# x^T k of the first attention layer by seven block products instead of eight full ones, its key sums on TensorE, and weight scans as flat rows

## The chip, the cores and the metric

The kernel runs on one core of one Trainium2 chip. The metric is the device time of one execution in microseconds; the time before is the median of three runs.

The core has five engines with a queue each: TensorE (PE; PEld is its weight load), VectorE (DVE), ScalarE (ACT), GpSimd (POOL) and SyncE (SP). DMA transfers are issued from the queues of SP, ACT and POOL. Each queue is worked off in program order.

## The reference

Four layers on one sequence of 2048 rows of 1024 features: linear attention (A), gated block (B), and the same two once more with the same weights.

```python
phi = lambda t: jnp.where(t > 0, t + 1, jnp.exp(t)) + 1e-6
# A, on layernorm(x):
q, k, v = x @ wqkv                       # 32 heads of 32
kv  = einsum("bhsd,bhse->bhde", phi(k), v)
z   = einsum("bhsd->bhd", phi(k))
num = einsum("bhqd,bhde->bhqe", phi(q), kv)
den = einsum("bhqd,bhd->bhq", phi(q), z) + 1e-6
x   = x + (num / den) @ wo
# B, on layernorm(x):
x   = x + ((x @ w_gate) * (x @ w_up)) @ w_down
```

## The kernel before

**Tiles.** The 2048 rows are 16 tiles of 128 (t). A product is a group of matmuls of 128 x 128 by 128 x 512 into PSUM. PSUM is eight banks, used as four pairs, QP[0] to QP[3]. The instructions of all engines are written out by hand in one program order, and the framework adds the waits for data and buffers. A step stands in the queue of each of its engines at the place where its call is made.

**kv without v.** k^T v is computed as (x^T k)^T wv: first x^T k, summed over all rows (1024 x 1024, held in XK), then its product with wv by blocks (kv_unit), masked to the heads. So v is never made.

**Layer A, first time (layer_A(0)).** The key stage makes phi(k) for the 16 tiles. For each tile: statistics on VectorE (ln_stats: bn_stats, bn_aggr, then two small POOL operations), the normed tile (ln_apply on VectorE, or ln_apply_act: a POOL operation for the offset, then ACT), its transposition by a DMA on SP (tx), 16 matmuls (k_tile), and phi: exp on ACT, min and max on VectorE, the last one from PSUM. `units` lists these steps, two half tiles (index i) per tile; the lines under `for i, (t, n)` place everything else by i.

Next, xk_pair(c) makes 128-row blocks of x^T k two at a time: 2 x 16 matmuls over all tiles, and one copy on ACT. There are eight. Meanwhile sum_unit adds up the 16 key tiles in float32 on VectorE (sk), and z_parts and z_unit turn that into the sum over all 2048 rows, repeated in every partition (zb), by a matmul with ones.

Then come the query tiles (q_tile). The first eleven are woven with the remaining xk_pairs. A query tile issues 16 matmuls into a pair of banks, phi, and some steps of `later`: den_sums (phi(q) times zb, summed per head) and den_divide, whose result is transposed by DMA for the output product. With split set, ACT also reads PSUM for the x + 1 side of phi, and VectorE reads SBUF alone. Then kv_unit, the last five query tiles with kvo_unit (kv times wo), and 16 output tiles (out_tile: 16 matmuls, one add to X on VectorE). `jobs` places the norms and other preparations for layer B between the output tiles.

**Layer A, second time (layer_A(2)).** It uses block products: a 2 x 2 block scheme with seven products instead of eight. x_product(p, jp, pair) issues half of product p (16 matmuls), xsums and tsums make the sums of blocks of x and of keys on VectorE in 16-bit, x_add adds a saved product to the one in PSUM, and ACT saves products 1, 6 and 7. Layer B works by the same scheme.

**Scales.** The 16-bit float format of the block sums needs scales for the weights. They are powers of two from the weights' sums of squares. scan_fetch loads 512 KB of w_gate, w_up or w_down, and scan_step squares it on ACT with a sum (42 of them); scale_sum, scale_pow (a matmul with ones for the sum over partitions), scale_root (POOL pow) and scale_bits make the factors fac, key_scale what phi of scaled keys needs. scan_key squares the key weights for the fourth factor. scan_buf gives each scan its buffer; a fetch waits until the square of the buffer's earlier scan is done.

**Down weights.** down_prep(u) loads a piece of w_down, scales it, makes its block sums and stores them (WD). Pieces 0 and 1 are made between output tiles, the rest in the first pass of layer B, one for each of its units.

Of the kernel before, what the change touches and what calls it, by code (L numbers as in the profile page):

```python
# [38 lines left out]
def kernel(  # L39
# [45 lines left out]
    QP = [QQ[:, 2 * i:2 * i + 2, :] for i in range(4)]  # L85
    WZ = [dram.tile([P, D + 64], F32, name=f"WZ{i}")[:, 0:D] for i in range(4)]
# [7 lines left out]
    def tail(i, j):  # L94
# [12 lines left out]
    sk = K[0][:, HEAD:HEAD + 2 * D].bitcast(F32)  # L107
# [6 lines left out]
    scan_b = [W[:, 6 * D:8 * D], K[0][:, HEAD:HEAD + 2 * D]]  # L114
    scan_c = [K[i][:, HEAD:HEAD + 2 * D] for i in (4, 0, 1, 2, 3)]
# [11 lines left out]
          for b in (K[3][:, 0:2 * D], K[3][:, 2 * D:4 * D], K[6][:, 0:2 * D], K[6][:, 2 * D:4 * D], W[:, 6 * D:8 * D])]  # L127
# [6 lines left out]
           for b in (K[0][:, HEAD:HEAD + 2 * D], MX[:, 2 * D:4 * D], W[:, 0:2 * D], W[:, 2 * D:4 * D], K[4][:, 0:2 * D])]  # L134
    sk2, zhi, zlo = MX[:, 2 * D:4 * D].bitcast(F32), W[:, 5 * D:6 * D], MX[:, D:2 * D]
# [66 lines left out]
    kq = const.tile([P, 4], F32, tag="kq", name="kq")  # L202
    kap = const.tile([P, 1], F32, tag="kap", name="kap")
    part = const.tile([P, 4], F32, tag="part", name="part")
    partb = const.tile([P, 4], BF16, tag="partb", name="partb")

    def scan_src(i):
        m, c = divmod(i, NU)
        if m < 2:
            f, kh = divmod(c, 2)  # L210
            return wgu_v[m][:, kh * KH:(kh + 1) * KH, f * NB:(f + 1) * NB], KH
        return wd_v[:, 2 * c:2 * c + 2, :], 2
# [3 lines left out]
    EARLY, MID = 26, 33  # L216
    scan_buf = [scan_a[i % 4] for i in range(18)] + [(scan_a + scan_b[:1])[i % 5] for i in range(18, EARLY)]
    scan_buf += [scan_b[(i + 1) % 2] for i in range(MID - EARLY)] + [scan_c[i % 5] for i in range(NSCAN - MID)]
    scanned = [0, 0, 0]

    def scan_fetch():

        while scanned[1] < scanned[2]:
            i = scanned[1]
            if any(scan_buf[j] is scan_buf[i] for j in range(scanned[0], i)):
                return
            src, k = scan_src(i)
            (nc.sync if i < 14 else nc.gpsimd).dma_start(out=scan_buf[i].rearrange("p (k n) -> p k n", k=k), in_=src)
            scanned[1] += 1

    def scan_step(n=1):

        for _ in range(n):
            i = scanned[0]
            m, c = divmod(i, NU)
            nc.scalar.activation(out=scan_buf[i], in_=scan_buf[i], func=ACT.Square, accum_out=acc[:, m, c:c + 1])  # L236
            scanned[0] += 1
            if i == EARLY - 1:
                load_qkv(wv, 2)
            elif i == EARLY - 2:  # L240
                scanned[2] = MID
            scan_fetch()

# [4 lines left out]
    def scale_pow(lo, hi):  # L248

        ps = mm_tile()  # L250
        nc.tensor.matmul(out=ps[:, lo:hi], lhsT=ones[:], rhs=partb[:, lo:hi], start=True, stop=True)
        nc.vector.tensor_scalar(out=part[:, lo:hi], in0=ps[:, lo:hi], scalar1=1e-30, scalar2=None, op0=ALU.max)
        if hi == 4:
            nc.vector.tensor_scalar(out=part[:, 3:4], in0=part[:, 3:4], scalar1=2.0 ** -10, scalar2=None, op0=ALU.max)
# [4 lines left out]
    def scale_bits(lo, hi):  # L259
# [6 lines left out]
        if hi == 4:  # L266
# [4 lines left out]
    def key_scale():  # L271
# [9 lines left out]
                                op0=ALU.mult, op1=ALU.add)  # L281

# [119 lines left out]

    def proj_mm(t, w, ps, mid=None, at=KD // 4):
# [21 lines left out]
    def xk_pair(c):  # L425

        n, j = divmod(2 * c, KD)
        bank = []

        def part(ts):  # L430
            if not bank:
                bank.append(mm_pair())
            for i in range(2):
                for t in ts:
                    nc.tensor.matmul(out=bank[0][:, i, :], lhsT=xn_a[t][:, (j + i) * P:(j + i + 1) * P],
                                     rhs=pk[t][:, n * NB:(n + 1) * NB], start=(t == 0), stop=(t == NT - 1))

        def end():
            part(range(NT - 2, NT))
            nc.scalar.copy(out=XK[n][:, j:j + 2, :], in_=bank[0])  # L440
        return [lambda: part(range(NT - 2)), end]

    def sum_unit(t):

        def run():
            nc.vector.tensor_tensor(out=sk, in0=pk[0] if t == 1 else sk, in1=pk[t], op=ALU.add)
        return run

    zparts = []

    def z_parts():

        hi = turn("pq", pqb)
        lo = turn("pq", pqb)
        nc.scalar.copy(out=hi, in_=sk)
        nc.vector.tensor_tensor(out=lo, in0=sk, in1=hi, op=ALU.subtract)
        zparts[:] = [hi, lo]

    def z_unit():
# [6 lines left out]
        nc.scalar.copy(out=halves(zb), in_=ps)  # L466

# [9 lines left out]
    def q_tile(t, split, mid=[], end=[], ring=4, done=2):  # L477
# [8 lines left out]
        pq = turn("pq", pqb) if eps[0] == 1e-6 else pqb[t % 4 if t < 6 else (4, 5, 0, 1, 2, 3)[t % 6]]  # L486
# [13 lines left out]
    eps = [1e-6]  # L500
# [11 lines left out]
    def den_sums(t, pq, den):  # L512
# [3 lines left out]
        if t % 2:  # L516
            nc.vector.tensor_scalar(out=den[:], in0=den[:], scalar1=eps[0], scalar2=None, op0=ALU.add)
# [67 lines left out]
    def key_stage(R, fill, xp):  # L585
# [8 lines left out]
        for u in range(NG + 1):  # L594
# [45 lines left out]
            if now:  # L640
                for t in range(TPG * (u - 1), TPG * u if was else 0):
                    nc.gpsimd.dma_start(out=WZ[t % 4], in_=pk2[t], **({"accum_op": ALU.add} if t > 3 else {}))
                if u == NG - 1:
                    for i, j in ((0, 1), (2, 3), (0, 2)):
                        nc.gpsimd.dma_start(out=WZ[i], in_=WZ[j], accum_op=ALU.add)
# [40 lines left out]
    def xsums(which, groups):  # L686
        for i, n in groups:
            a11, a12, a21, a22 = (xspan(i, l, h, n) for h, l in ((0, 0), (0, 1), (1, 0), (1, 1)))
            s2 = SX[:, i:i + n, :] if n > 1 else SX[:, i, :]
            o, a, b, op = {"S3": (a21.bitcast(F16), a11, a21, ALU.subtract), "S2": (s2, a22, a21.bitcast(F16), ALU.subtract),  # L690
# [3 lines left out]
    def tsums(which, pairs):  # L694
        for i in pairs:
            b11, b21, b12, b22 = (pk2[2 * i + l][:, n * NB:(n + 1) * NB] for n in range(2) for l in range(2))
            t2 = TY[:, i, :]
            o, a, b, op = {"T3": (b12, b22, b12, ALU.subtract), "T2": (t2, b12, b11, ALU.add),
# [680 lines left out]
```

## Time and profile before

| | us |
|---|---|
| median of 3 runs (1478.70 to 1479.68) | 1479.42 |
| profiled execution | 1479.06 |
| its span | 1477.3 |
| TensorE busy in it | 1468.1 |
| VectorE, ACT, POOL busy | 1044.1, 740.1, 111.2 |
| key stage ends, first x^T k matmul | 68.17 |
| first matmul of kv_unit | 162.50 |
| first matmul of layer B | 242.42 |

A line of the profile's timeline gives the start of a piece of work in the span, its length, the engine, the line of the kernel, the operation, output and inputs by buffer names, shape, and how many instructions were merged. In brackets stands the idle time of the engine before it and what ended it. The list of waits gives for each waiting engine and line what it waited for, the microseconds in total, how often, and the longest. The granted TensorE clock is 1.00 throughout.

### The profile page before, as it was taken

The page shows a single profiled execution, that of the slowest core. Times are in us where ns is not written, and L with a number is a line of the kernel's source. Part 1 is how long each engine was busy: PE and PEld are TensorE (multiplying, and loading weights), DVE is VectorE, ACT ScalarE, POOL GpSimd, SP SyncE. Part 2 cuts the span into 40 slices and gives each one's busy share as a digit, 9 for nine tenths or more (in the row PEclk, how much of TensorE's full clock was granted, in tenths as well). Part 3 has the DMA queues.
Part 4 walks back from the last instruction along what each step waited for, and adds up shares of the span by engine and source line. Part 5 has one row for each costly group of instructions (what it writes and reads, how often), then busy time and mean ns, then how long its engine had stood idle before and what let it go on. Part 6 is the DMA issues. An engine that isn't in the chain of part 4 may idle for free. (4 is left out here: it accounts for less than half of the span.)

```text
span 1477.3 us, 17671 instructions
## 1 busy us (share of the span) xinstructions
PE 1468.1 (99%) x6933; PEld 669.2 (45%) x6933; DVE 1044.1 (71%) x1510; ACT 740.1 (50%) x696; POOL 111.2 (8%) x239
## 2 busy tenths in 40 slices
PE   9999999999999999999999999999999999999999
PEld 4444544444444444444444445444444444444444
DVE  7856888888865477777389779777776746777532
ACT  5987695777601366540086336556663015666200
POOL 2121121000000000001042000200000100000000
PEclk9999999999999999999999999999999999999999
DMA  7866956777656333335649253453333853333442
GB/s 216 199 202 193 260 135 183 209 209 205 199 183 188 86 86 86 86 128 168 196 107 248 44 157 72 82 118 86 86 86 115 237 160 93 87 86 86 156 166 85
DMA packets 272532, 213.23 MB, mean 144 GB/s; under 512 B 102081, under 2 KB 257217, under 8 KB 268865
## 3 DMA queue, kind: packets, MB, share of 16 engines
q1 hardware_dynamic: 261232, 182.61, 44.4%
q0 software_dynamic: 6912, 25.17, 6.0%
q10 hardware_dynamic: 4304, 4.33, 0.9%
q8 instruction: 54, 0.88, 0.2%
q14 instruction: 30, 0.24, 0.0%
HBM read 162.53 MB, written 27.00 MB: 128 GB/s over the span
## 5 line engine op out<-in xcount | busy, mean ns | idle before, releaser
L896 PEld LDWEIGHTS <-K 128*128 128x128 f16 x3136 | 306.8, 98 | 370.0
L896 PE MATMUL Q<-XT,K 128*128 128x512 bf16 (+1 forms) x1792 | 405.7, 379 | 0.0
L1198 PE MATMUL Q<-K,K 128*128 128x512 f16 (+2 forms) x1582 | 340.4, 377 | 0.0
L896 PE MATMUL Q<-TX,K 128*128 128x512 f16 x1344 | 308.4, 379 | 0.0
L858 ACT ACTIVATE K<-K,fac 128x2048 f16<-128x2048 bf16 x112 | 224.7, 2009 | 128.0 <-DMA K<-in_B_w_gate_dram 128.0
L1198 PEld LDWEIGHTS <-K 128*128 128x128 f16 x1582 | 154.3, 98 | 184.5
L861 DVE TENSOR_TENSOR K<-K 128x1024 f16<-128x1024 f16 (+1 forms) x244 | 156.9, 665 | 103.8 <-ACT K L858 101.8
L861 DVE TENSOR_TENSOR W<-MX,Q 128x1024 f16<-128x1024 f32 x88 | 107.3, 1220 | 38.4 <-PE Q L896 19.6
L916 ACT COPY MX<-Q 128x1024 f32<-128x1024 f32 x60 | 60.8, 1013 | 123.5 <-PE Q L896 110.9
L861 DVE TENSOR_TENSOR W<-W,Q 128x1024 f16<-128x1024 f32 x80 | 97.6, 1220 | 17.9 <-PE Q L896 13.5
L916 ACT COPY W<-Q 128x1024 f32<-128x1024 f32 x52 | 52.7, 1013 | 92.6 <-PE Q L896 79.9
L861 DVE TENSOR_TENSOR K<-K,K 128x512 f16<-128x512 f16 (+1 forms) x148 | 87.7, 597 | 4.2
L409 PE MATMUL Q<-K,K 128*128 128x512 bf16 x384 | 87.0, 379 | 1.9 <-DMA K<-K 1.6
L409 PE MATMUL Q<-K,XT 128*128 128x512 bf16 x384 | 86.0, 379 | 0.6 <-ACT XT L379 0.4
L900 DVE TENSOR_TENSOR K<-W 128x512 f16<-128x512 f16 x168 | 71.3, 425 | 5.8
L392 ACT ACTIVATE W<-Q 128x1024 bf16<-128x1024 f32 (+1 forms) x52 | 49.1, 949 | 46.2 <-PE Q L409 46.2
L236 ACT ACTIVATE K<-K 128x2048 bf16<-128x2048 bf16 x37 | 70.3, 1905 | 0.7 <-DMA K<-in_B_w_down_dram 0.6
L1212 DVE SCALAR_TENSOR_TENSOR W<-Q,kap,X 128x1024 f32<-128x1024 f32 x16 | 20.5, 1284 | 66.3 <-PE Q L1198 66.3
L301 POOL TENSOR_SCALAR ve<-mv 128x1 f32<-128x1 f32 x45 | 11.3, 251 | 720.1 <-DVE mv L299 719.6
L913 ACT COPY MX<-Q 128x1024 f32<-128x1024 f32 x28 | 28.3, 1010 | 72.7 <-PE Q L896 72.7
L295 DVE BATCH_NORM_STATS2 st<-X 128x6 f32<-128x512 bf16 x92 | 58.2, 673 | 2.6 <-DMA X<-in_A_x_dram 2.5
L409 PEld LDWEIGHTS <-K 128*128 128x128 bf16 x384 | 37.1, 98 | 48.0 <-DMA K<-K 3.6
(196 smaller groups left out, 1368.3 us busy)
## 6 DMA issues: line engine op xcount, KB each, us to landing
K<-WD SPq DMA_DIRECT2D x28, 1792.0 KB, 7.3
K<-in_B_w_gate_dram SPq DMA_DIRECT2D x70, 512.0 KB, 4.1
K<-in_B_w_up_dram SPq DMA_DIRECT2D x56, 512.0 KB, 5.1
K<-in_A_wqkv_dram SPq DMA_DIRECT2D x10, 1024.0 KB, 8.2
WZ<-K POOLq DMA_DIRECT2D x16, 512.0 KB, 6.4
K<-in_B_w_down_dram POOLq DMA_DIRECT2D x12, 512.0 KB, 5.6
K<-in_B_w_up_dram POOLq DMA_DIRECT2D x11, 512.0 KB, 5.2
K<-in_B_w_down_dram SPq DMA_DIRECT2D x10, 512.0 KB, 5.3
```

The lines of the kernel that those rows point to most:

```text
L236: nc.scalar.activation(out=scan_buf[i], in_=scan_buf[i], func=ACT.Square, accum_out=acc[:, m, c:c + 1])
L295: nc.vector.bn_stats(out=stat[t][0][:, c, :], in_=X[:, t, c * NB:(c + 1) * NB])
L392: nc.scalar.activation(out=e, in_=ps, func=ACT.Exp)
L409: nc.tensor.matmul(out=ps, lhsT=xt[:, k, tl * P:(tl + 1) * P], rhs=w[:, k, :], start=(k == 0), stop=(k == KD - 1))
L858: nc.scalar.activation(out=b.bitcast(F16), in_=b, func=ACT.Copy, scale=fac[:, m:m + 1])
L861: eng.tensor_tensor(out=o, in0=a, in1=b, op=op)
L896: nc.tensor.matmul(out=pair[:, m, :], lhsT=stationary(n, p, m, k), rhs=moving[p][:, k, :], start=(p in (1, 2, 5) and k == 0), stop=(k == K ...
L900: nc.vector.tensor_tensor(out=hA[i][:, u, :], in0=gu[:, 0, :], in1=gu[:, 1, :], op=ALU.mult)
L913: nc.scalar.copy(out=snaps[u, 1], in_=a)
L916: nc.scalar.copy(out=snaps[u, p], in_=a)
L1198: nc.tensor.matmul(out=ps_[:, lo:hi], lhsT=act[:, u, j * P:(j + 1) * P], rhs=w[:, u, lo:hi], start=(p in (1, 2, 5) and u == 0), stop=(u == ...
L1212: stt(out=o, in0=ps_, scalar=kap[:, 0:1], in1=x, op0=ALU.mult, op1=ALU.add)
```

## The change

It touches the first attention layer, its scales, and where the down weights are prepared.

- **x^T k.** xk_pair is gone. xq_first issues products 1, 2, 6, 7, 5, 4, 3 in two halves each, with the query tiles 0 to 10 between them. The sums of x blocks (S1 to S4) and of key blocks (T1 to T4) are formed in place, with another choice of sums than in the second layer.
- **Scaled keys.** Block sums of keys are taken of keys in 16-bit float times the key scale. So the key scale is made early. scan_key runs right after the first units. The sum over partitions no longer goes through a matmul: the column of 128 sums is written to DRAM (WS) and read back as a row in each partition, both on SP, then summed on VectorE. Keys of tiles 7 to 15 are made scaled (phi_scaled), those of tiles 0 to 6 are multiplied later (key_scaled).
- **Key sums.** sum_unit and z_parts are gone for this layer. z_sums adds the block sums over all rows on TensorE (16 matmuls with ones) and finishes with two copies and one add.
- **Scans.** A scan reads w as flat rows: each partition a run of 2048 neighbouring elements. None runs in the key stage any more, four are fetched near its end. The first 16 fetches are on SP, the rest on POOL; from scan 24 on at most three are ahead.
- **Other moves.** w_v is loaded in halves from ACT's queue after scans 21 and 23; wq at i = 21; the last four x tiles at i = 5 instead of 2. Tiles 13 and 15 are normed on VectorE. Down pieces 0 and 1 move into layer B's first pass, where units 2 and 4 take two pieces, and all but piece 0 are scaled on ACT. Between output tiles, norms of tiles 0 to 3 are on VectorE, those of 4 to 6 on ACT. In both layers A conversions and one weight load sit at other output tiles, and products of the second layer take the tile pairs in groups of 4, 2, 2 instead of 6, 2.

```diff
     def scan_src(i):
         m, c = divmod(i, NU)
-        if m < 2:
-            f, kh = divmod(c, 2)
-            return wgu_v[m][:, kh * KH:(kh + 1) * KH, f * NB:(f + 1) * NB], KH
-        return wd_v[:, 2 * c:2 * c + 2, :], 2
+        return flat[m][:, c * SW:(c + 1) * SW]
...
-            if any(scan_buf[j] is scan_buf[i] for j in range(scanned[0], i)):
+            if any(scan_buf[j] is scan_buf[i] for j in range(scanned[0], i)) or i >= max(EARLY, scanned[0] + 3):
                 return
-            src, k = scan_src(i)
-            (nc.sync if i < 14 else nc.gpsimd).dma_start(out=scan_buf[i].rearrange("p (k n) -> p k n", k=k), in_=src)
+            (nc.sync if i < SYNC else nc.gpsimd).dma_start(out=scan_buf[i], in_=scan_src(i))
...
+    def phi_scaled(ps, t):
+
+        e, x1 = halves(turn("e", eb)), halves(turn("x1", pb)).bitcast(F16)
+        nc.scalar.activation(out=e, in_=ps, func=ACT.Exp, bias=lnk[:])
+        nc.scalar.activation(out=x1, in_=ps, func=ACT.Identity, scale=fac[:, 3:4], bias=kq[:, 1:2])
+        nc.vector.tensor_scalar(out=e, in0=e, scalar1=fac[:, 3:4], scalar2=kq[:, 2:3], op0=ALU.min, op1=ALU.add)
+        nc.vector.tensor_tensor(out=halves(pk2[t]), in0=x1, in1=e, op=ALU.max)
...
+    def z_sums():
+
+        ps = mm_pair()
+        for n, l in ((1, 0), (0, 1)):
+            for i in range(8):
+                nc.tensor.matmul(out=ps[:, n, :], lhsT=ones[:], rhs=pk2[2 * i + l][:, n * NB:(n + 1) * NB],
+                                 start=(i == 0), stop=(i == 7))
+        nc.scalar.copy(out=z2[:], in_=ps[:, 1, :])
+        nc.scalar.copy(out=zb[:, NB:], in_=ps[:, 1, :])
+        nc.vector.tensor_tensor(out=zb[:, 0:NB], in0=z2[:], in1=ps[:, 0, :], op=ALU.add)
...
+                if i == 2:
+                    nc.vector.tensor_reduce(out=part[:, 3:4], in_=acc[:, 3:4, :], axis=AX.X, op=ALU.add)
+                elif i == 3:
+                    nc.sync.dma_start(out=WS[:, :], in_=part[:, 3:4])
+                elif i == 6:
+                    nc.sync.dma_start(out=row, in_=WS[:, :].rearrange("p o -> o p").to_broadcast([P, P]))
+                elif i == 8:
+                    nc.vector.tensor_reduce(out=part[:, 3:4], in_=row, axis=AX.X, op=ALU.add)
+                    nc.vector.tensor_scalar(out=part[:, 3:4], in0=part[:, 3:4], scalar1=2.0 ** -10, scalar2=None, op0=ALU.max)
+                    scale_root(3, 4)
+                elif i == 9:
+                    scale_bits(3, 4)
+                    key_scale()
+                do(key_jobs.get(i, []))
...
+    def xq_first():
+        a0, a1, b0, b1 = 3, 0, 1, 2
+
+        def q(t, i, done):
+            at_pair(i)
+            q_tile(t, t > 6, done=done)
+
+        for pairs in (range(6), range(6, 8)):
+            for jp, i in ((0, a0), (1, a1)):
+                x_mm(1, jp, QP[i], pairs)
+        scan_step(2)
+        x_end(1, 0, QP[a0])
+        x_end(1, 1, QP[a1])
+        scan_step(2)
+        tsums("T3", range(4))
+        x_product(2, 0, QP[b0])
+        x_add(2, 0, QP[b0])
+        scan_step(2)
+        x_product(2, 1, QP[b1])
+        xsums("S2", XG)
+        x_add(2, 1, QP[b1])
+        tsums("T3", range(4, 8))
+        tsums("T2", range(8))
+        q(0, b0, 0)
+        q(1, b1, 0)
+        x_product(6, 0, QP[a0])
+        scan_step(1)
+        xsums("S4", XG)
+        x_product(6, 1, QP[a1])
+        scan_step(1)
+        xsums("S3", XG)
+        tsums("T4", range(8))
+        tsums("T1", range(8))
+        q(2, b0, 0)
+        scan_step(1)
+        x_product(7, 0, QP[a0])
+        scan_step(2)
+        x_product(5, 0, QP[b1])
+        at_pair(b0)
+        z_sums()
+        x_add(5, 0, QP[b1])
...
+        q(4, a0, 3)
+        at_pair(b0)
+        z_column()
+        scan_step(1)
+        x_product(7, 1, QP[a1])
+        scan_step(2)
+        x_product(5, 1, QP[b1])
+        x_add(5, 1, QP[b1])
+        scan_step(1)
+        q(5, b0, 3)
...
+        scanned[2] = MID
+        scan_fetch()
+        q(7, b0, 2)
...
+        q(10, b0, 2)
+        load_o()
+        scan_step(1)
+        at_pair(a0)
```

## The prediction

> **What bounds the kernel now.** I read the page's first part, the chain that ended last, the list of waits on TensorE, TensorE's timeline through the first attention layer, and a table of busy time by stretch.
>
> The page: span, share of the span per engine, and where the last chain runs.
>
> ```profile
> span 1477.3 us, 17671 instructions
> PE 1468.1 (99%) x6933; PEld 669.2 (45%) x6933; DVE 1044.1 (71%) x1510; ACT 740.1 (50%) x696; POOL 111.2 (8%) x239
> ...
> PE 39%; DVE 0%; issue 0%
> ```
>
> TensorE is idle for 1477.3 - 1468.1 = 9.2 us in all, and the chain is TensorE alone. What counts is the number of matmuls, and any hole that opens between them. TensorE's timeline has start, length, line and count:
>
> ```profile
> 49.29 7.18 PE L409 MATMUL Q<-K,K 128*128 128x512 bf16 x32 [0.53 <-DMA K<-K]
> 57.52 10.82 PE L409 MATMUL Q<-K,K 128*128 128x512 bf16 x48 [1.04 <-DMA K<-K]
> 68.17 1.46 PE L435 MATMUL Q<-K,TX 128*128 128x512 bf16 x6
> ...
> 162.50 3.74 PE L810 MATMUL Q<-K,K 128*128 128x128 bf16 x64
> ```
>
> The two holes (1.57 us) are key tiles 11 and 13 waiting for their transposed activations. From 68.17 to 162.50 stand the old x^T k, eleven query tiles and the key sums: 256 + 176 + 4 = 436 matmuls and eight tiny ones, so 94.33 us, 0.2159 us a matmul, without a hole. The list of waits of TensorE from 60 to 260 us has one entry:
>
> ```profile
> PE Q L409 <- DVE W L401: 0.2, 1, 0.2
> ```
>
> How full the other engines are (stretch, length, PE, PEld, DVE, ACT, POOL busy, clock, DMA share, GB/s):
>
> ```profile
> 50.00:60.00 10.00, 8.96 (x42) 3.80 (x41) 9.00 (x15) 9.93 (x11) 3.30 (x9) 1.00 1.00 204
> ...
> 88.90:115.00 26.10, 26.10 (x130) 11.93 (x129) 10.14 (x13) 20.85 (x22) 6.73 (x9) 1.00 0.65 199
> ```
>
> In the key stage ACT is full and DMA saturated: that is why transposes are late. In the stage that is rewritten, this stretch leaves ACT 20% and VectorE 61%. ACT's timeline of the key stage shows its cycle, a norm, a key square, an exp and another square until the next norm, 4.12 us for a tile that TensorE does in 3.45:
>
> ```profile
> 35.40 1.23 ACT L322 ACTIVATE ST<-X,off,rstd 128x1024 bf16<-128x1024 bf16 x1
> 36.53 1.04 ACT L286 ACTIVATE W<-K 128x1024 bf16<-128x1024 bf16 x1
> ...
> 37.57 1.00 ACT L392 ACTIVATE W<-Q 128x1024 bf16<-128x1024 f32 x1
> 38.48 1.04 ACT L286 ACTIVATE W<-K 128x1024 bf16<-128x1024 bf16 x1
> ...
> 39.52 1.23 ACT L322 ACTIVATE K<-X,off,rstd 128x1024 bf16<-128x1024 bf16 x1
> ```
>
> **What the Trainium skill says.** "TensorE: Matmul & The Clock Gate", Back-to-back issue gap: a warm 512-column matmul every N/2.4 + 2.5 = 216 ns; the trace has 215.9. "VectorE: DVE Perf Modes", The perf-mode tier table: tensor_tensor on 16-bit data in SBUF at twice the base rate, with PSUM at the base rate, tensor_scalar at four times. The trace agrees: 1.22 us for 2048 16-bit elements, 1.22 for 1024 from PSUM, 0.76 for a 2048 tensor_scalar. "DMA: Bandwidth & Descriptors", Queues, rings and completion order: each DMA engine consumes a ring's descriptors in order, so a small transfer stands behind large ones issued before it; no run here shows it yet. Same page, Anatomy of one DMA: about 2 us fixed per transfer; the shortest landing on the page is 1.5 us (32 KB of output).
>
> **The change, part by part.** Steps (start to start) are from the second layer, which already multiplies by seven products: 512-element 16-bit sum 0.34, a full set of block sums over keys (8) 2.75, over x 2.47, x_add from PSUM 1.14; ACT exp 0.91, identity 1.01, copy 0.91, a scan square 1.90; phi on VectorE 1.67 unsplit, 1.12 split. VectorE's timeline there, first x sum, first key sums, next operation (825.35 - 822.88 = 2.47, then 2.75 to 828.10):
>
> ```profile
> 822.88 0.95 DVE L692 TENSOR_TENSOR TX<-K,TX 128x1536 f16<-128x1536 f16 x1
> ...
> 825.35 0.75 DVE L700 TENSOR_TENSOR K<-K 128x512 f16<-128x512 f16 x2
> 826.02 2.09 DVE L700 TENSOR_TENSOR K<-K,K 128x512 f16<-128x512 f16 x6
> 828.17 0.43 DVE L397 TENSOR_SCALAR W<-W 128x1024 bf16<-128x1024 bf16 x1
> ```
>
> *TensorE.* Eight pairs of 32 matmuls become fourteen half products of 16 (224, minus 32); z_unit's 4 become z_sums' 16 (plus 12). Net minus 20, at 0.2159: **-4.32 us**, a stage of 90.0 us. One more one-column matmul in scale_pow: nothing.
>
> *Key stage* (to 68.17 before). Gone from it: ACT's eight key squares at one per unit (moved to 10-26 us, where ACT idled 5.1 us waiting for POOL's off), six scan squares, thirteen 512 KB scan loads on SP, four key sums on VectorE. Hence ACT falls from 4.12 us a tile to about 2 (3 from tile 7), below TensorE's 3.45. Added: the key scale, in queues that the norms use. By hand: the moved squares delay norm(6) by 0.35 us, harmless. norm(8) starts 31.6, tx(8) goes out on SP at 32.9, behind it now the four x loads (0.5 us each, to 36.2), then the row broadcast at 36.3, then tx(9), in time (needed 41.7). Loads of x landed in 3.2 to 3.7 us in this stretch: row lands about 39.2. VectorE reaches reduce(row) at 38.7 and waits 0.5; behind it wait key_scale, ln_stats(11) and all later phi. The sum and floor take 0.4; POOL's pow 0.6-0.8 stands ahead of off(10) on POOL: off(10) at 40.7, norm(10) to 41.9, transposed in 3.2: 45.2 against 45.15 needed. scale_bits and key_scale (nine tiny ops; six took 0.62) hold VectorE to 41.5. From there VectorE paces the norms: per tile 1.40 statistics, 1.12 phi_scaled and two key_scaled of 0.45 (half the 0.76 row, rounded up) = 3.4 against 3.45, plus norm(13) 0.5. Following that queue: norm(14) ends at 57.0, lands 60.3, needed 59.0. So a hole of about 1.3 us at tile 14, for the 1.57 that go: **-0.3 us**. Bounds: -1.6 (no hole) to +2.5 (row 2 us later, landings of 4 us).
>
> *x^T k and q stage*, time from its start. VectorE: key sums 4 x 2.75, x sums 3 x 2.47, six x_add 6.8, phi 16.2, den_sums 18.6 (1.86 and 2.79 in turn), den_divide 9.1, z 0.9: 70 of 90 us. ACT: 28 scans 53, exp and identity 14, copies 8: 76 of 90. Both fit; the order decides. Product 6 starts at 20.7 and needs T2, done 19.4; 7 starts at 31.1, needs S3, 28.4; 5 at 34.5, T1's first pair 31.6; z_sums at 38.0 needs phi(q2) off its bank, 35.7. So 1.3 to 2.9 us of cover each. The one place without: q(5) takes z_column's bank at 62.5, while the reciprocal that frees it stands behind phi(q4), two divisions and a den_sums and ends at 63.0: **+0.5**. The wv halves now go out on ACT's queue behind squares 21 and 23, at 69 and 76, and take 8.2: 84 for a need at 90. wq goes out at about 55 instead of 69.6, needed at 82. Scans: the buffer ring is four, refill 5.5 us after the square; from the ninth on they arrive about 2 us early. Scan 24 is fetched when product 3 ends (76.0), lands 82.2, ACT wants it at 82.4. ACT then runs 2 us behind; identity(q10) ends 93.8 and q(11), in the same bank after only kv_unit, starts 94.2: **+0.3** for a cover that thin (0 to 1.5).
>
> *Query/output tiles and later.* Out tile 0's add ends about 10 us after the last query tile as before (9.5), but scale_pow takes a bank, so out_tile(3) needs it at 10.6: **+0.3** (0 to 1). VectorE takes three more norms of 1.95 (5.9 us) into six out tiles that leave it idle about 2 us each (1.93, 2.23, 2.00); without that cover the four t_fill sums would be late by as much. dp[0], dp[1] leave this stage and pair up in units 2 and 4 of the first gate pass: VectorE 10.1 + 1.35 of 12.09, ACT 9.1 + 2.0: fits. Moved load_unit(1,1) still has 6.9 us before its conversion. Second-layer edits reorder equal work: 0.
>
> Sum: -4.3 - 0.3 + 0.5 + 0.3 + 0.3 = -3.5. The profiled execution took 1479.06 (span 1477.3 and 1.76 around it), 0.36 under the median 1479.42. From the median: **1475.9 us**.
>
> **Rivals.** *Holes vanish* (tile 14's transposition also arrives in time, as DMA is quiet): -4.3 - 1.6 + 0.5 = 1474.0. For it: ACT relieved, no scan loads; against: VectorE at 3.4 of 3.45.
> *ACT or VectorE paces the new stage:* a refill later than 5.5 us makes ACT late at every exp, or sums run late by more than 1.3 us. For: ACT 84% full, against 80% in the row above. Two or three more holes of about 1.3 us: 1479, no measurable change.
> *Slower: the row arrives late.* Tile 10 starts 6.0 us after the row lands, one for one beyond 39.1. Landing at 42.6 eats the gain; beyond 45.6 the kernel is slower by over 0.2%. Fetched as 16384 single words it would: 92 transposes make most of the 102081 packets under 512 B, some 1100 each in about 1.1 us of DMA time (the table's only busy microsecond at 26-27 has share 1.11), so 16 us more, an estimate: about 1490. Against: 128 neighbours in DRAM are one 512 B run.
>
> **Chances.** Forecast 0.50 (its own range 1474.3 to 1477.9; 0.38 of it below 1476.5), no holes 0.14, paced stage 0.18 (0.02 of it slower), late row 0.18 (0.01 of it still inside). A measurement of this kernel tells 0.2%, 3.0 us, from no change. Faster 0.38 + 0.14 = 0.52; slower 0.02 + 0.17 = 0.19; same the remaining 0.29. Range 1473.3 (no holes, with a little less elsewhere) to 1484.5 (a row near 47 us).
>
> **What would show it.** TensorE's stage between the last key tile and kv_unit is 90.0 us plus holes, with 416 matmuls. The row sum on VectorE starts near 39 us with a wait on DMA; a hole near tile 14; a short wait on the reciprocal of z_column; none on scan loads. I am wrong if holes before 160 us exceed 5 us in total, or if ACT waits for scan data more than once.

## The result, and the profile after

The changed kernel took 1489.24 us (median of 4 runs, 1488.19 to 1491.42) against 1479.55 for the kernel before beside it: a ratio of 1.0068, interval 1.005 to 1.0085. It is slower by 9.7 us, where 3.5 us less were forecast.

The page of the changed kernel, span, busy time and the chain that ended last:

```profile
span 1488.0 us, 17649 instructions
PE 1469.0 (99%) x6913; PEld 668.1 (45%) x6913; DVE 1056.5 (71%) x1577; ACT 744.5 (50%) x693; POOL 103.3 (7%) x230
...
PE 39%; DVE 0%; issue 0%
```

The 20 matmuls are gone (6933 before, 6913 after), yet TensorE is busy 0.9 us longer and idle 19.0 us instead of 9.2. Its list of waits to 260 us names where; the three largest:

```profile
PE Q L932 <- DMA TX<-in_A_wo_dram: 5.3, 1, 5.3
PE Q L419 <- DMA K<-ST: 2.2, 1, 2.2
PE Q L419 <- ACT W L408: 1.9, 2, 1.7
```

One wait is on wo ahead of the kvo products, one on the transposition of key tile 8, and the third holds the one forecast at tile 14. TensorE's timeline of the key stage and around kv_unit:

```profile
40.85 8.77 PE L419 MATMUL Q<-K,K 128*128 128x512 bf16 x32 [2.20 <-DMA K<-ST]
50.14 3.63 PE L419 MATMUL Q<-K,K 128*128 128x512 bf16 x16 [0.52 <-DMA K<-K]
...
67.00 7.08 PE L419 MATMUL Q<-K,K 128*128 128x512 bf16 x32 [1.67 <-ACT W L408]
73.92 0.81 PE L726 MATMUL Q<-K,TX 128*128 128x512 f16 x3
...
136.90 3.61 PE L419 MATMUL Q<-K,XT 128*128 128x512 bf16 x16 [0.45 <-DVE rz L464]
...
164.52 3.74 PE L922 MATMUL Q<-K,K 128*128 128x128 bf16 x64
174.02 0.38 PE L932 MATMUL Q<-ST,W 128*128 128x512 bf16 x1 [0.59 <-DMA ST<-in_A_wo_dram]
...
179.70 0.61 PE L932 MATMUL Q<-TX,W 128*128 128x512 bf16 x1 [5.30 <-DMA TX<-in_A_wo_dram]
180.10 3.62 PE L419 MATMUL Q<-K,K 128*128 128x512 bf16 x8
...
184.37 2.17 PE L419 MATMUL Q<-K,K 128*128 128x512 bf16 x8
186.38 0.38 PE L932 MATMUL Q<-ST,W 128*128 128x512 bf16 x1
```

The stage that was rewritten runs from 73.92 to 164.52, 90.60 us with one hole of 0.45. After the large holes the same work takes longer: 32 matmuls in 8.77 us at 40.85, 7.08 at 67.00; 8 in 3.62 at 180.10, where 1.89 is usual, and slow up to 186.38. The table by stretch gives the clock as its third number from the right:

```profile
41.00:46.00 5.00, 5.00 (x16) 1.90 (x15) 0.95 (x8) 0.21 (x1) 0.81 (x2) 0.66 0.80 227
46.00:51.00 5.00, 4.48 (x21) 1.86 (x20) 4.76 (x14) 3.38 (x4) 1.11 (x3) 1.00 0.28 54
...
180.00:185.00 5.00, 5.00 (x13) 1.82 (x12) 0.00 (x0) 1.50 (x2) 0.00 (x0) 0.51 1.12 318
```

What stood in front of tile 8 is on SP's queue, and behind it on VectorE and ACT. The timeline of these, the sum's way over DRAM and who waits for it:

```profile
30.60 0.53 SPq L1191 DMA_DIRECT2D WS<-part  x1
33.24 1.77 SPq L347 DMA_TRANSPOSE K<-ST  x1
39.65 0.33 SPq L1193 DMA_DIRECT2D W<-WS  x1
...
44.29 0.29 DVE L1195 TENSOR_REDUCE part<-W 128x1 f32<-128x128 f32 x1 [4.95 <-DMA W<-WS]
...
45.78 1.24 ACT L324 ACTIVATE K<-X,off,rstd 128x1024 bf16<-128x1024 bf16 x1 [8.23 <-POOL off L322]
```

The write WS of 128 words went out at 30.60 and landed 9.0 us later. SP stood behind it with the broadcast read, which landed 4.6 us after 39.65. The transposition of tile 8, issued between them, landed 7.6 us after 33.24; the middle of the key stage's transpositions is 3.1.

Where the 10.7 us between the two spans lie, and the experiments that were timed several times by the same marks (us between the first matmuls of the stages; ratio to the kernel before beside it, with its interval). The marks are those of one profiled execution each. For g4 it is the longest of five, 1487.13, where the others took 1482.76 to 1483.38.

| kernel | median | ratio | to first x^T k | to kv_unit | to output tiles | to layer B | to the end |
|---|---|---|---|---|---|---|---|
| before | 1479.55 | | 68.17 | 94.33 | 24.64 | 55.28 | 1234.9 |
| after | 1489.24 | 1.0068 (1.005 to 1.0085) | 73.92 | 90.60 | 33.08 | 55.28 | 1235.1 |
| e1 | 1487.0 | 1.0051 (1.0034 to 1.0067) | 74.56 | 90.59 | 28.85 | 55.28 | 1236.0 |
| e2 | 1490.17 | 1.0075 (1.006 to 1.0091) | 72.19 | 90.59 | 32.80 | 55.28 | 1235.9 |
| e3 | 1483.55 | 1.0026 (1.0015 to 1.0038) | 72.71 | 90.60 | 28.79 | 55.37 | 1236.1 |
| e4 | 1480.34 | 1.0005 (0.9997 to 1.0014) | 68.47 | 94.33 | 25.78 | 55.28 | 1235.1 |
| q1 | 1486.39 | 1.0058 (1.0041 to 1.0075) | 70.10 | 90.59 | 31.67 | 55.27 | 1235.4 |
| q2 | 1486.78 | 1.0052 (1.0037 to 1.0067) | 70.05 | 90.60 | 35.17 | 55.28 | 1234.9 |
| g1 | 1490.9 | 1.008 (1.0065 to 1.0095) | 69.85 | 90.59 | 26.60 | 67.65 | 1235.0 |
| g2 | 1490.18 | 1.0077 (1.006 to 1.0094) | 69.54 | 90.59 | 26.74 | 66.56 | 1234.9 |
| g3 | 1478.18 | 0.9995 (0.9986 to 1.0003) | 69.55 | 90.59 | 24.80 | 56.63 | 1234.8 |
| g4 | 1483.24 | 1.003 (1.0018 to 1.0043) | 73.55 | 90.60 | 29.34 | 56.62 | 1235.3 |
| g5 | 1479.6 | 1.0003 (0.9995 to 1.0011) | 71.12 | 90.59 | 24.88 | 55.34 | 1235.8 |
| g6 | 1478.36 | 0.9996 (0.9987 to 1.0004) | 69.45 | 90.59 | 24.69 | 55.55 | 1236.3 |

So the change gained 3.73 in the stage it rewrote, and lost 5.75 in the key stage ahead of it and 8.44 around wo behind it.

### The profile page after: what moved, and what is told of

It reads as the page before. It is cut to its first block, busy times and chain, and to the rows that moved or that the text cites. A ratio compares the mean times of both kernels' runs of the same rounds, so it can differ in the third digit from the quotient of the medians.

```text
span 1488.0 us, 17649 instructions
## 1 busy us (share of the span) xinstructions
PE 1469.0 (99%) x6913; PEld 668.1 (45%) x6913; DVE 1056.5 (71%) x1577; ACT 744.5 (50%) x693; POOL 103.3 (7%) x230
## 5 line engine op out<-in xcount | busy, mean ns | idle before, releaser
L419 PE MATMUL Q<-K,K 128*128 128x512 bf16 x384 | 90.5, 391 | 5.1 <-DMA K<-ST 2.2
L237 ACT ACTIVATE K<-K 128x2048 bf16<-128x2048 bf16 x42 | 79.9, 1907 | 5.4 <-DMA K<-in_B_w_down_dram 3.4
L394 ACT ACTIVATE W<-Q 128x1024 bf16<-128x1024 f32 (+1 forms) x43 | 40.3, 940 | 49.4 <-PE Q L419 49.2
L297 DVE BATCH_NORM_STATS2 st<-X 128x6 f32<-128x512 bf16 x98 | 62.0, 674 | 3.0 <-DMA X<-in_A_x_dram 2.9
```

The lines of the kernel that those rows point to most:

```text
L297: nc.vector.bn_stats(out=stat[t][0][:, c, :], in_=X[:, t, c * NB:(c + 1) * NB])
L394: nc.scalar.activation(out=e, in_=ps, func=ACT.Exp)
L419: nc.tensor.matmul(out=ps, lhsT=xt[:, k, tl * P:(tl + 1) * P], rhs=w[:, k, :], start=(k == 0), stop=(k == KD - 1))
```

## The experiments

**The places of the row and of wo.** Theory at this point: wo is late because its load stands behind q(10), and the key stage is late because VectorE stands for the row. e1 moves wo, e2 the row, e3 both; e4 puts wo late in the kernel before.

```diff
 e1, e3            x_add(3, 1, QP[b1])
+                  load_o()
                   scanned[2] = MID
 ...               q(10, b0, 2)
-                  load_o()
 e2, e3  -  elif i == 8:     # sum of the row, root
         +  elif i == 10:
         -  elif i == 9:     # scale_bits, key_scale
         +  elif i == 11:
 e4: in the kernel before, load_o() from t == XT_ - 2 to behind the last q_tile of that loop
```

> The changed kernel with the two loads of wo issued right behind product 3's second half, before query tile 7, instead of behind query tile 10. Theory A (the loads are issued 14 us too late, and the hole at the first kvo product restarts TensorE at a lower clock): the 5.9 us of waiting on wo and some 2 us of slow matmuls behind it go; 1489.2 falls by 7.5 to 8.5, to about 1481. Rival B (DMA is saturated there, so wo, wv and the scans only change places): wo arrives in time but wv or scan 24 comes late, and less than 4 us are won, 1485 to 1489.

> The changed kernel with the sum of the row, the root and the key scale read two units later (i = 10 and 11 for 8 and 9), nothing else. Theory A (VectorE stands on the row that lands at 44.2 us, and POOL's offset for tile 10 stands behind its root): VectorE waits under 2 us instead of 5.0, norm(10) goes out before the row, holes of the key stage fall from 5.0 to about 2 us and the slow matmuls behind the first one (1.7 us) go with the hole that makes them; about 1485. Rival C (VectorE at 3.4 us a tile paces the norms anyway, and transposes are late for the DMA's sake): the holes move to later tiles, under 1.5 us won.

> Both edits together: wo early and the row read later. If the two causes are separate and each is what theory A says, the gains add: 1489.2 - 8 - 4 = about 1477, below the kernel before (1479.5). If they share a cause (DMA as a whole), the sum is clearly smaller, 1481 or more.

> The kernel before with one move alone: the two loads of wo issued behind query tile 10 instead of before query tile 9. Theory A: issued near 166 instead of 160.5, the second half lands at 174 to 180 against 171.6 needed; a hole of 3 to 8 us and slow matmuls behind it, 1484 to 1489. Rival B (only the new stage's loads make wo late): 1480 to 1482.

e1, then e2, on TensorE:

```profile
171.30 7.03 PE L419 MATMUL Q<-K,K 128*128 128x512 bf16 x23 [2.41 <-ACT W L398]
```

```profile
42.28 22.58 PE L419 MATMUL Q<-K,K 128*128 128x512 bf16 x94 [3.54 <-DMA K<-ST]
```

e1 took 4.2 us off the wo stretch and not more: nothing waits for wo, but q(11) now waited 2.41 us for ScalarE, and the clock behind that hole was low again. So the time is as rival B said, and the cause is neither theory's. e2 shows that the row is not what holds tile 8: with nobody waiting early for the row, the hole ahead of tile 8 stayed (3.54; 3.22 in e1, whose key stage is that of the changed kernel), the key stage got back only 1.7, and the median did not fall. e3 adds both, and its ScalarE timeline shows why q(11) is late (the second load of wo, the next exponential):

```profile
150.28 5.82 ACTq L161 DMA_DIRECT2D TX<-in_A_wo_dram  x1
156.20 1.02 ACT L394 ACTIVATE W<-Q 128x1024 bf16<-128x1024 f32 x1 [7.05 <-issue]
```

Issuing that load held ScalarE for 5.82 us, where the loads before it took 0.65 or less; the exponential and all behind it came late, with a hole of 2.66 us at 169.70. e4 says that the late place alone costs little. Its wo hole is 0.90 us, and in its trace no scan piece is issued between 156 and 169 us:

```profile
173.26 0.38 PE L820 MATMUL Q<-TX,W 128*128 128x512 bf16 x1 [0.90 <-DMA TX<-in_A_wo_dram]
```

**The write of 128 words.** Theory D: this write is slow by itself and holds up what is around it. Rival T: the loads of x, moved in the changed kernel to right behind it, make it slow. In the d kernels the write is added to the kernel before and read by nobody; x1 puts the loads of x back.

```diff
 d1 (source acc), d3 (source mhalf, as below), in the kernel before
+                if i == 3:
+                    nc.sync.dma_start(out=WS[:, :], in_=mhalf[:, 0:1])
 d4: WS is [P, 128], out=WS[:, 0:1]     d5: WS is [P, 16], out=WS[:, 0:1]
 d6: out=WS[0:32, :], in_=mhalf[0:32, 0:1]
 x1, in the changed kernel
-                if i == 5:
+                if i == 2:
                     for x in range(3 * TPG, NT): load_x(x)
```

> The kernel before with nothing added but one write of 128 words of 4 bytes from 128 partitions into 512 successive bytes of DRAM, on SP behind the loads of x, at the place of the changed kernel's write; nobody reads it. Theory D (the write of single words itself is slow and holds up the transfers around it): it takes 7 to 11 us to land, the transposition issued behind it takes 5 us or more where the others take 3 to 4, and the first x^T k matmul comes 1 to 4 us after 68.2. Rival T (in the changed kernel the write was slow because the four loads of x were issued just behind it): it lands in 2 to 4 us, the transposition behind it in 3 to 4, and the first x^T k matmul stays within 0.7 us of 68.2.

> The changed kernel with only the loads of x(12) to x(15) put back to where the kernel before issues them, three units earlier, ahead of the write of the key sums and of the transposition of tile 8. Theory D: the write still takes 7 us or more and the hole ahead of tile 8 on TensorE stays above 1 us; key stage ends 71.5 to 74. Rival T: the write lands in 2 to 4 us, the hole ahead of tile 8 goes (2.2 us), the row of sums lands by 40, the first x^T k matmul comes at 68.5 to 70, and the time falls to 1484.

> The kernel before with one added write of 128 words of 4 bytes into 512 successive bytes of DRAM, on SP behind the loads of x, now from a constant that nothing writes afterwards (in the write of acc before, ScalarE's later sums into acc had to wait for it, 12.9 us). Theory D: it lands in 8 to 11 us, the transposition behind it in 5 us or more, and the first x^T k matmul comes 1 to 4 us after 68.2. Rival W (the write is slow, but harms nothing that does not wait for it): it lands in 8 to 11 us, the transposition behind it in 3 to 4 us, and the first x^T k matmul stays within 0.7 us of 68.2.

> The same added write with its 128 words 512 bytes apart in DRAM. If the words are slow because they fall into the same 512 bytes: it lands in 2 to 4 us and the transposition behind it in 3 to 4. If each word is slow by itself, wherever it goes: it lands in 8 to 11 us as in the packed one.

> The kernel before with the added write of 128 words, now 64 bytes apart in DRAM (10.5 us to land packed, 4.3 us at 512 bytes). If words in different stretches of 64 bytes don't hold each other up: 4 to 5 us, transpositions behind it 3 to 5.5, first x^T k matmul below 69.2. If the stretch that counts is longer than 64 bytes: between the two or as packed, first x^T k matmul 70 or later.

> The kernel before with the added write of 32 words from partitions 0 to 31 into 128 successive bytes. If the words queue one behind another at one place in DRAM (128 words 10.5 us, some 4.3 us of it there without queueing, so some 50 ns a word): 5 to 6.5 us. If the packed write has a fixed price whatever its words: 8 to 11 us. If few words are hidden: 2 to 4.5 us.

In d1 the write took 10.2 us, but ScalarE's sums into acc had to wait for it, so its time of 1492.02 belongs to that wait. In x1 it took 10.5 us with the loads of x ahead of it, and the key stage ended at 76.95, later than the 71.5 to 74 that D gave: T falls. d3 is the clean case. TensorE's timeline, then the table by stretch (the last two numbers are DMA share and GB/s):

```profile
42.97 30.44 PE L410 MATMUL Q<-K,K 128*128 128x512 bf16 x125 [4.18 <-DMA K<-ST]
73.47 1.46 PE L436 MATMUL Q<-K,TX 128*128 128x512 bf16 x6
```

```profile
34.00:36.00 2.00, 2.00 (x10) 0.74 (x9) 0.61 (x2) 2.00 (x4) 0.84 (x2) 1.00 1.04 200
36.00:38.00 2.00, 2.00 (x11) 0.89 (x10) 2.00 (x3) 2.00 (x4) 0.00 (x0) 1.00 1.48 34
38.00:40.00 2.00, 0.79 (x4) 0.18 (x2) 1.34 (x4) 2.00 (x5) 1.08 (x3) 1.00 0.79 31
40.00:42.00 2.00, 0.00 (x0) 0.00 (x0) 1.97 (x4) 2.00 (x4) 0.00 (x0) 0.99 0.59 16
```

From 36 us on the DMA engines are shown busy, with shares of 1.48 to 0.59, and move 16 to 34 GB/s. One 1 KB read of a weight scan took 8.9 us in the trace; in the kernel before none from 28 to 46 us took over 0.7. The write landed after 10.5 us, and the three transpositions issued from 33 to 44 us after 9.8 to 11.2. The first x^T k matmul came 5.3 us after the kernel before's, for an operation that nothing reads: nearly the 5.75 of the changed kernel. d5's same stretch shows the reads flowing:

```profile
36.00:38.00 2.00, 2.00 (x10) 0.94 (x11) 2.00 (x3) 2.00 (x4) 0.00 (x0) 1.00 0.88 221
38.00:40.00 2.00, 2.00 (x11) 0.89 (x10) 1.35 (x4) 2.00 (x4) 1.07 (x3) 1.00 1.13 215
```

| write added to the kernel before | landed after | transpositions issued 29 to 45 us, at most | first x^T k | one run, us |
|---|---|---|---|---|
| d3: 128 words side by side | 10.5 | 11.2 | 73.47 | 1484.61 |
| d6: 32 words side by side | 7.3 | 6.9 | 68.33 | 1481.46 |
| d5: 128 words 64 bytes apart | 4.3 | 5.4 | 68.32 | 1479.82 |
| d4: 128 words 512 bytes apart | 4.3 | 5.4 | 68.89 | 1480.55 |

Each of these was run once. The two 128-word writes with gaps and d6 left the key stage's end within 0.7 us of the kernel before, so d3's 5.3 us stand clear; d6's longer time arose behind the first matmul of layer B (1237.1 us to the end, against 1234.9), where nothing was changed. It is not the smallness of the words, nor their number alone, but many of them close together. For d6, 5 to 6.5 us were forecast and 7.3 measured, so the price is not in proportion to the words.

**Without the way over DRAM.** q1 makes the sum over partitions on VectorE: a 32x32 transposition of the broadcast sums, a sum, and six copies between groups of partitions. q2 also issues wo on SP, right behind x_add(3, 1).

```diff
                 if i == 2:
                     nc.vector.tensor_reduce(out=part[:, 3:4], in_=acc[:, 3:4, :], ...)
-                elif i == 3:
-                    nc.sync.dma_start(out=WS[:, :], in_=part[:, 3:4])
-                elif i == 6:
-                    nc.sync.dma_start(out=row, in_=WS[...])
+                    nc.vector.tensor_copy(out=tq[:, 0:32], in_=part[:, 3:4].to_broadcast([P, 32]))
+                    nc.vector.transpose(out=tq[:, 32:64], in_=tq[:, 0:32])
+                elif i == 3:   # sq[:, 0:1] = sum of tq[:, 32:64]; copies a -> a ^ 1, 32 partitions each
+                elif i == 4:   # sq[:, 2:3] = sum of both; copies of 64 partitions
+                elif i == 5:   # part[:, 3:4] = sum of both
                 elif i == 8:
-                    nc.vector.tensor_reduce(out=part[:, 3:4], in_=row, axis=AX.X, op=ALU.add)
                     ...
```

> The changed kernel with the way over DRAM taken out: the key sum over the partitions is made on VectorE by a 32x32 transposition, a sum and six copies between groups of 32 partitions, so that neither the write nor the broadcast read exists. Theory D: transposition of tile 8 lands in 3 to 4 us, no wait for a row, the first x^T k matmul at 68 to 69.5 instead of 73.9, and the time falls by 4 to 6 us to 1483 to 1485 (the hole of the wo load stays at 5 to 7 us). Rival K (the key stage is late by its own VectorE and ScalarE work, not by the way over DRAM): first x^T k matmul at 71.5 or later, time 1487 to 1489.

> As the kernel with the sum on VectorE, and the two loads of wo issued on SP's queue (nothing is queued there at that time) right behind x_add(3, 1) instead of on ScalarE's behind q(10), so that ScalarE isn't held by their issue. If the two causes (the way over DRAM, the late wo) are the whole of the loss: no hole over 1 us in either place, span 1474.5 to 1476, median 1475.5 to 1478, ratio 0.9975 to 0.999. Rival B (q(10) and q(11) share a bank, and the wait for its reading is 1.5 us or more also without the held ScalarE): a hole of 1.5 to 2.7 us ahead of q(11), median 1478 to 1480. Rival M (memory traffic makes wo late wherever it is issued): a hole of 2 us or more ahead of the kvo products, 1480 or more.

q1's key stage on TensorE, to be held against 73.92:

```profile
46.35 3.63 PE L420 MATMUL Q<-K,K 128*128 128x512 bf16 x16 [0.89 <-DMA K<-K]
50.62 10.97 PE L420 MATMUL Q<-K,K 128*128 128x512 bf16 x47 [0.64 <-DMA K<-K]
63.18 6.86 PE L420 MATMUL Q<-K,K 128*128 128x512 bf16 x31 [1.59 <-ACT W L409]
70.10 0.81 PE L727 MATMUL Q<-K,TX 128*128 128x512 f16 x3
```

The hole at tile 8 and the low clock are gone, 3.8 us, though the stage ends at 70.1, later than the 68 to 69.5 expected. Three holes of 3.1 us in all remain, without any way over DRAM. As the timelines show it, the first two end on transpositions whose norms ScalarE began 2.88 and 1.62 us late, for offsets that follow VectorE's statistics; the third ends on ScalarE's exponential. q2 failed for its queue. The transpositions of the divided query tiles go out on SP, and stood behind wo there, one of them landing 19.2 us after its issue; VectorE waited for a buffer that one of them read:

```profile
173.72 0.69 DVE L402 TENSOR_TENSOR MX<-W 128x1024 bf16<-128x1024 bf16 x1 [8.62 <-DMA XT<-MX]
```

**Order of wo and the scan pieces.** From q1 on: wo on GpSimd's queue ahead of the four scan pieces fetched there, so that it goes first without blocking anyone; the scans that ScalarE did at q(7) to q(10) have to move. g2 adds the normalisation of tile 14 on VectorE. g3 places the moved scans anew, g4 is g3's wo and scans in the changed kernel with its way over DRAM, g5 and g6 trim g3.

```diff
 g1, g2   x_add(3, 1, QP[b1])
+         load_o(nc.gpsimd)
          scanned[2] = MID; scan_fetch()
-         scan_step(1) behind each of q(7) to q(10) and q(11), and load_o()
+         scan_step((1, 1, 2, 1)[i]) in the kvo stage, 13 in the output tiles, scale_sum(0, 2) at i == 3
 g2 to g6 but g4: - (ln_apply_act if t < 13 or t == 14 else ln_apply)
                  + (ln_apply_act if t < 13 else ln_apply)
 g3, g4 against g1: scan_step(3) behind q(10), 1 behind q(11), 1 at i == 2 and at i == 3,
                    12 in the output tiles, scale_sum at i == 1
 g5 = g3 with no scan at i == 2, 13 in the output tiles, and scale_bits, key_scale at i == 10 for 9
 g6 = g5 with these back at i == 9
```

> The kernel with the key sum on VectorE, with the loads of wo issued on GpSimd's queue right behind x_add(3, 1) and ahead of the four scan pieces fetched there (the pieces come behind wo on the same queue), and the five scans of q(7) to q(11) moved into and behind the kvo stage, so that ScalarE waits for none of them. Theory T (wo was late because the scan pieces and wv shared the transfers with it): no hole above 0.7 us ahead of the kvo products, first kvo to first output tile 24.5 to 26 us, span 1475.5 to 1477.5, median 1477 to 1479.5. Rival P (it is the place of wo's own transfers ahead of the kvo stage, 2 MB there whatever the order): a hole of 2 us or more remains there, on wv, on wo or on a transposition, 1480 or more.

> The same, and the normalisation of tile 14 on VectorE, as that of 13's neighbours 13 and 15, in place of ScalarE, which stood 3.5 us for its offsets with the exponentials of tiles 10 to 13 behind it. Theory: the hole of 1.6 us ahead of tile 14 on TensorE goes or halves, the first x^T k matmul comes at 68.6 to 69.5 instead of 70.1, and the median is 0.5 to 1.5 us below that of the run with wo first. Rival: VectorE, busy from 42 to 72 us, becomes late by the same: hole stays above 1 us, no gain.

> The key sum on VectorE, tile 14 normalised on VectorE, wo on GpSimd's queue ahead of the scan pieces; against the run before it, three of the five moved scans go back behind q(10) and one behind q(11), where ScalarE stood 5.0 us for TensorE and the pieces have landed (159.5 to 164.7), so that the kvo stage carries two scans and the output tiles twelve. If the loss was the late wo and the way over DRAM: first x^T k matmul 69.5, first kv product 160.1, first output tile 185 to 186.5, first layer B matmul 240.5 to 242, span 1475.5 to 1477, median 1476.5 to 1479, ratio 0.998 to 0.9995: the 4.3 us of the removed matmuls then show less some 2 us that the key stage is later than before. Rival S (the scans have no place left: ScalarE is what bounds the kvo stage and the output tiles in the changed kernel): holes of 1 us or more on ScalarE's KVo copies or on partb, 1480 or more.

> The changed kernel with only the edit on wo and the scans of the run before it (the key sum goes over DRAM as in the changed kernel). If the two causes are apart from one another: first x^T k matmul 73.5 to 75, first kv to first output tile 25 to 26.5 instead of 33.1, median 1481 to 1484. If the wo hole only came from the late key stage or goes elsewhere: 1486 or more.

> The run before it (sum on VectorE, wo first) with two edits: the scan that stood on ScalarE ahead of the last two KVo copies (183.7 us, holes of 0.40 and 0.63 on TensorE behind it) goes behind the twelve in the output tiles, and the bits and factors of the key scale come one unit later on VectorE, so that VectorE doesn't stand 0.66 us for GpSimd's root and the statistics of tile 10 come about 1.9 us sooner (hole of 1.03 ahead of tile 10). If both holes go: first x^T k matmul at 68.5 to 69.2, first layer B matmul 239.5 to 240.5, span 1474.3 to 1475.5, median 1476 to 1477.5, ratio 0.998 to 0.9987. Rival: the thirteenth scan makes the normalisations ahead of layer B late (a hole of 1 us or more ahead of the first layer B matmul), 1478 to 1479.5.

> The run with wo first and the scans placed (1478.2 us), with only the first of the two last edits: the scan ahead of the last two KVo copies goes behind the twelve in the output tiles; the key scale stays where it was. In the run with both edits the output tiles took 55.34 us for 56.63, and the key stage 1.57 us more (ScalarE's first scaled exponential waited for the later factors, a hole of 2.04). If the two add up: first x^T k matmul 69.5, first layer B matmul 240.2 to 240.6, span 1475 to 1475.6, median 1476.5 to 1477.5, ratio 0.998 to 0.999. Rival: the gain of 1.3 us is given back in layer B, whose first products then wait for VectorE (0.77 there in the run with both): 1478 to 1479.

g1 answers its question and loses the time elsewhere. No hole on wo is left, and the stretch to the output tiles falls from 31.67 to 26.60, but the moved scans now stand between ScalarE's copies of KVo, and TensorE waits for those and for the sums:

```profile
191.82 0.57 PE L939 MATMUL Q<-K,XT 128*128 128x512 bf16 x1 [3.54 <-ACT K L930]
...
200.30 0.19 PE L254 MATMUL Q<-partb,ones 128*128 128x2 bf16 x1 [4.18 <-DVE partb L249]
```

g2's hole at tile 14 fell from 1.59 to 0.42, but one of 0.52 opened ahead of tile 15: 0.3 us in sum. g3 puts the scans where ScalarE stood for q(11): 24.80 to the output tiles, and only short waits are left, on VectorE once and on ScalarE's last copies.

```profile
169.62 0.38 PE L930 MATMUL Q<-TX,W 128*128 128x512 bf16 x1 [0.20 <-DVE W L922]
...
187.80 2.10 PE L940 MATMUL Q<-K,XT 128*128 128x512 bf16 x9 [0.63 <-ACT K L931]
```

g4, with the DRAM way left in, is at 1483.24, 6 us below the changed kernel. In its profiled execution, the longest one, wv was late instead (a hole of 3.20; its second load landed 18.5 us after issue); for the other four this isn't shown. Against the kernel before beside each, the medians of q1, g4 and g3, which has both repairs and the norm of tile 14 on VectorE, lie 2.3, 5.9 and 11.0 us better than the changed kernel's. g5's scan edit worked (55.34 for 56.63), but its later key scale made ScalarE's scaled exponentials late (a hole of 2.04). g6 drops that and starts layer B 2.1 us before the kernel before; from there to the end it takes 1.4 us longer, with one hole seen:

```profile
245.09 1.90 PE L1006 MATMUL Q<-TX,K 128*128 128x512 f16 x8 [1.20 <-DVE TX L971]
```

g3 and g6 stand 1.3 and 0.65 us below the kernel before in the medians, with intervals that hold 1: the repaired change is no measurable gain, and no version here clearly beats the kernel before. The 3.74 us of the rewritten stage are there in both, but g3 loses 1.38 of them in the key stage and 1.35 between the output tiles, g6 1.28 in the key stage and 1.4 from layer B on.

## Why the prediction was wrong

The saving on TensorE came as forecast. What failed are three terms that the sum put at nothing: the landing of the write ahead of the row, the later loads of wo, and the low clock behind a hole.

**TensorE, -4.32, and the xq stage: right.** 90.60 us were measured; the forecast was 90.0, plus 0.5 for the reciprocal of z_column (0.45, on that very wait) and 0.3 for q(11). The 0.3 did not show in the changed kernel; in e1 and e3 the same cover gave way, with holes of 2.4 and 2.7. Output tiles: 0.3 forecast, 0.0. Later layers: 0 forecast, 0.2.

**The key stage, -0.3: wrong, the step that failed is "row lands about 39.2".** That step took a DMA's landing from the loads of x, 3.2 to 3.7 us, for a read whose data had still to be written: the write had no term of its own. It took 9.0 us. The page "DMA: Bandwidth & Descriptors" of the Trainium skill, Anatomy of one DMA, gives about 2 us fixed per transfer for DMAs on GpSimd's path; the prediction carried that over to SP's queue, and it did not cover this. d5's 4.3 us is the nearest that this write comes to it. "128 neighbours in DRAM are one 512 B run" was offered against the late row; for the write it is the very reason, as d3 against d5 shows. The rival of the late row was nearer: its rule that tile 10 starts 6.0 us after the row gives 44.2 + 6.0 = 50.2, and it did at 50.14. But its cause was the read as single words, 16 us more, and the read landed in 4.6, so that the row came late by the write: the agreement is luck. Nor was it the row that cost most: holes of 2.20 ahead of tile 8 and 1.70 us of low clock behind it came from the transposition of tile 8 that landed late behind the write. The forecast sent it out at 32.9 and gave it no landing at all ("in time" is said there of tile 9's).

Of the 5.75 lost, q1 gives back 3.8 with the way over DRAM. Most of the remaining 1.9 is the forecast's other error: q1 has holes of 3.1 us, where before 1.57 stood. The prediction followed VectorE's queue to one hole of 1.3 at tile 14, and missed those ahead of tiles 10 and 11 (0.89 and 0.64). At tile 14 the size is near (1.59 in q1), the wait is another: what ended last was not the transposition but ScalarE's exponential, which stood behind the norm of tile 14.

**wo: no term at all.** The prediction worked out wv's new loads and left out that load_o moves behind q(10). The loads went out 4.2 us later (164.73 for 160.54), and landed 9.3 and 14.5 us after issue instead of 5.3 and 9.3. The second load and the landings of the two, in the changed kernel and in the kernel before:

```profile
L161 ACTq DMA_DIRECT2D TX<-in_A_wo_dram x1: 595/595/595, 165.1 to 165.1; - x1
...
DMA to landing us min/median/max: 9.3/11.9/14.5
```

```profile
L159 ACTq DMA_DIRECT2D TX<-in_A_wo_dram x1: 595/595/595, 161.0 to 161.0; - x1
...
DMA to landing us min/median/max: 5.3/7.3/9.3
```

Holes of 5.89, and 2.4 of low clock (18 matmuls from 180.10 to 186.38, 6.28 us for 3.89), make 8.3 of the 8.44. e1 (the early place with the changed kernel's traffic, no wait on wo) and e4 (the late place without it, 0.90) put the blame on place and traffic together. That the traffic is the scan pieces is read from the timelines, and was not tested apart: the kernel before issues none there, the changed one a piece every 3.8 us.

**The clock behind a hole: no term.** The prediction counted a hole at its own length. Behind the holes of 2.20 and 5.30 us in the changed kernel the low clock cost 1.7 and 2.4 us more, behind d3's 4.18 it cost 2.9 (128 matmuls in 30.50 us for 27.64).

Both signs named as proof of error came true. "Holes before 160 us exceed 5 us in total": 5.04 in the key stage and 0.45. "ACT waits for scan data more than once": 1.92 us at 78.4 and 3.44 at 215.9, though no hole on TensorE followed from either.

## What to carry to other kernels

A value that goes over DRAM has two landings, and the write's must be priced by where its words fall: 128 neighbouring words of four bytes took 9.0 to 10.5 us to land and slowed the other traffic meanwhile, 64 bytes apart 4.3. When a load is moved, list what is in flight at its new place and what stands behind its issue on the queue; the edit that looks like bookkeeping lost more here than the mathematics gained. A saving of 4 us needs every other edit in the change to stay under 4 us together, so test the parts one by one.

## What the runs showed of the hardware

- A 128-word write into 512 successive bytes of DRAM slowed other reads of DRAM (a 1 KB packet 8.9 us in d3) and made transpositions from SBUF to SBUF land late (9.8 to 11.2 us in d3, 5.4 at most in d4 and d5). Tile 8's transposition had its last packets at 36 us in the changed kernel, and landed at 40.8. "DMA: Bandwidth & Descriptors", Queues, rings and completion order, says that a completion count lands only after every earlier write of its DMA engine; that would explain it, and was not tested apart. The same page's Specifications say that transfers under 512 bytes are read, modified and written; d4 and d5 show that this alone was not the price.
- Issuing a 1 MB load held ScalarE for 5.82 us in e3 and 5.58 in e1, when three such loads were issued on its queue within 1.1 us; the changed kernel's took 0.59.
- TensorE's clock fell to 0.50 behind a hole of 2.20 us (changed kernel) and 0.51 behind one of 5.30, and not behind one of 3.06 (x1: 16 matmuls in the usual 3.63). So the length of a hole alone did not decide it. "TensorE: Matmul & The Clock Gate", on the clock gate, gives half the clock after an idle window of some 3.4 us that runs freely; the halving agrees, and a hole shorter than that was enough here.
